# k weights as column halves around x of tile 3, a column of ones in the normalised tiles, and v weights less their row 512

## The chip, the cores and the metric

The kernel runs on one core of a Trainium2 chip. The metric is the device time of one execution in microseconds, as the median of several runs. Profiles come from one further execution that the hardware profiler recorded.

## The reference

The input x has 2048 rows of 640 values in bfloat16. The result is x plus two branches, and the second branch itself contains x again:

```python
def _A_ref(x, wqkv, wo):              # linear attention, 32 heads of 20
    qkv = (x @ wqkv) ...              # q, k, v
    phi = lambda t: jnp.where(t > 0, t + 1, jnp.exp(t)) + 1e-6
    pq, pk = phi(q), phi(k)
    kv = jnp.einsum("bhsd,bhse->bhde", pk, v)
    z = jnp.einsum("bhsd->bhd", pk)
    num = jnp.einsum("bhqd,bhde->bhqe", pq, kv)
    den = jnp.einsum("bhqd,bhd->bhq", pq, z)[..., None] + 1e-6
    return (num / den) ... @ wo

def _B_ref(x, w_r, w_gate, w_up, w_down):
    r = x @ w_r                       # the 8 rows of largest r go through
    idx = argsort(-r)[:8]             # a gated MLP, scaled by sigmoid(r)
    y = (silu(x[idx] @ w_gate) * (x[idx] @ w_up)) @ w_down * sigmoid(r[idx])
    return x + scatter_add(idx, y)

xn = _layernorm(x)
return x + _A_ref(xn, A_wqkv, A_wo) + _B_ref(xn, B_w_r, B_w_gate, B_w_up, B_w_down)
```

The layernorm has no gain and no bias: the 640 values of a normalised row add up to zero, apart from rounding.

## The kernel before

**Tiles.** The rows form 16 tiles of 128 (`T`), the 640 columns five chunks of 128 (`KC`). `XX[:, t, 1, :]` holds x of a tile, `XX[:, t, 0, :]` the normalised tile, `xnT` the normalised rows transposed, `pk` the feature map of k, `pqT` that of q, transposed. All of PSUM is one tile `PS` of eight banks, given out by hand.

**Engines and queues.** The order on each engine is the order of the program text (`manual_schedule`); waits between engines and for DMAs are derived from the tiles' accesses. PE multiplies, ACT does exponentials and copies, DVE the statistics, normalisation and elementwise work, POOL a square root for each tile (`ln_s`), masks and the gather of the selected rows. SP's queue issues nearly all loads and stores (`ld(sp, ...)`) and the DMA transposes (`tr_dma`).

**Start.** SP issues x of tiles 0, 1, 2, then the k weights `wk` in two parts, chunks 0 to 2 and 3 to 4, then x of tile 3 and of the rest. PE runs zero matmuls (`warm`) and transposes the router weights `w_r`, which ACT copies into column 640 of `wk` (L362, L364): so the second half of K also yields the router logits, 321 columns instead of 320. Tiles 0 to 3 are transposed on PE (`tr_pe`), later ones by DMA.

**k phase** (L339 to L445). `K(t)` multiplies tile t by the k weights in two halves of 320 columns (banks 6 and 7, ten matmuls), `PHa` takes exp and relu on ACT, `PHb` joins them into `pk` on DVE. `G(t)` (L261) accumulates G = xn^T pk over all tiles in banks 0 to 5, with the last 128 by 128 block done apart (`corner`, bank 6). The v projection isn't computed by rows: kv is later made from G and the v weights `wv` (`kv_pe`), in blocks along the diagonal. Iteration t of the loop runs K(t), PHb(t-1), the normalisation of tile t+2 with its DMA transpose, statistics of tile t+3 (`ln_a`, `ln_b`, `ln_g`, `ln_s`, `ln_c`), then G(t-1) and `loads(t)`: the q weights in five loads at 7 to 11, and at 13 the v weights in one, output weights, gate and up weights.

**q phase** (L465 to L825). `q_pe(tb, m, bank)` computes 128 columns of q for 512 rows, ACT takes exp and relu at once, `q_fin` joins them on DVE. Between these blocks stand: G's copies to SBUF, the routing of the eight rows (`route1` to `route3`), `kv_pe` and the masked evictions `kv_ev`, `zsum` (the sums of pk over all rows, by 64 matmuls with a tile of ones, into bank 2), `z_ev` and `z_mask`, which spread z over partitions, `m_tiled` and `m_full` (kv times the output weights), `den` (the denominators), the MLP (`gu_pe`, `ht_pe`, `y_pe`). `wd`, the down weights, uses the memory of `pk`, so it is loaded after pk's last reader.

**Output phase.** `out_mm(t)` and `out_ev(t)` for 16 tiles; the MLP's rows are added in DRAM by indirect DMAs.

Of the kernel before, what the change touches and what calls it, by code (L numbers as in the profile page):

```python
# [7 lines left out]
P = 128  # L8
S = 2048
D = 640  # L10
# [3 lines left out]
T = S // P  # L14
KC = D // P
# [8 lines left out]
EPS_BF16 = 1.0013580322265625e-05  # L24
LOW = S - 1
TF = 11

# [9 lines left out]
def kernel(  # L37
# [27 lines left out]
    def st(shape, dt, name, tag=None):  # L65
        return sb.tile(shape, dt, name=name, tag=tag or name)
# [4 lines left out]
    pqT = st([P, KC, S], BF16, "pqT")  # L71
    wk = st([P, KC, D + 1], BF16, "wk", "wkM")
    wq = st([P, KC, D], BF16, "wq")
# [21 lines left out]

    HW = 320


    def ld(eng, dst, src):
        eng.dma_start(dst, src)  # L100
# [8 lines left out]
    ld(sp, XX[:, 2, 1, :], x_v[:, 2, :])  # L109
    ld(sp, wk[:, 0:3, 0:D], wqkv_v[:, 0:3, D : 2 * D])  # L110
    ld(sp, wk[:, 3:KC, 0:D], wqkv_v[:, 3:KC, D : 2 * D])


    def warm(n, w=512):
        for _ in range(n):
            pe.matmul(PS[:, 7, 0:w], lhsT=zero[:, 0:P], rhs=zero[:, 0:w], start=True, stop=True)
# [40 lines left out]

    def ln_act(t):
        act.activation(junk[:], XX[:, t, 1, :], AF.Identity, scale=1.0 / D, accum_out=sm[:, t, 0:1])
        act.copy(MV[:, t, 0:1], sm[:, t, 0:1])  # L160
        act.activation(junk[:], XX[:, t, 1, :], AF.Square, scale=float(D) ** -0.5, accum_out=sm[:, t, 1:2])

    def ln_var(t):
# [55 lines left out]

    def K(t, hs=(0, 1), b=6, kcs=range(KC)):  # L220
        for h in hs:
            w = HW + h
            for kc in kcs:
                pe.matmul(  # L224
                    PS[:, b + h, off(t, h) : off(t, h) + w],
                    lhsT=xnT[:, kc, t * P : (t + 1) * P],
                    rhs=wk[:, kc, h * HW : h * HW + w],
                    start=(kc == 0),
                    stop=(kc == KC - 1),
                )  # L230
# [6 lines left out]
    def PHe(t, h, b=6):  # L237
        if h == 0:
            phis[t] = tuple(tmp.tile([P, D], BF16, tag=k, name=k, bufs=3) for k in ("ek", "rk"))
        act.activation(phis[t][0][:, h * HW : (h + 1) * HW], phi_src(t, h, b), AF.Exp)  # L240

    def PHr(t, h, b=6):
        act.activation(phis[t][1][:, h * HW : (h + 1) * HW], phi_src(t, h, b), AF.Relu)  # L243

# [12 lines left out]
    def PHb(t):  # L257
        ek, rk = phis[t]
        dve.scalar_tensor_tensor(out=pk[:, t, :], in0=ek[:], scalar=1.0, in1=rk[:], op0=ALU.min, op1=ALU.add)  # L259

    def G(t, ks=range(KC)):  # L261
        for a in ks:
# [5 lines left out]
            if a < 4:  # L268
# [3 lines left out]
                )  # L272

    def corner(t):
        pe.matmul(
            PS[:, 6, 0:P], lhsT=XX[:, t, 0, 512:D], rhs=pk[:, t, 512:D],
            start=(t == 0), stop=(t == T - 1), skip_group_check=True,
        )

    def zsum(b):  # L280
        for t in range(T):
            for j in range(4):
                pe.matmul(PS[32 * j : 32 * j + 32, b, 0:GC], lhsT=ones32[:], rhs=pk[:, t, j * GC : (j + 1) * GC],
                          start=(t == 0), stop=(t == T - 1), skip_group_check=True)

# [37 lines left out]
    def loads(t):  # L323
        if t < 5:
            ld(sp, XX[:, 6 + 2 * t : 8 + 2 * t, 1, :], x_v[:, 6 + 2 * t : 8 + 2 * t, :])
        if 7 <= t < 7 + KC:
            ld(sp, wq[:, t - 7, :], wqkv_v[:, t - 7, 0:D])
        if t == 13:
            ld(sp, wv[:], wqkv_v[:, :, 2 * D : 3 * D])
            ld(sp, wo1[:], wo_v[0:P, :, :])  # L330
            for g in range(NG):
                ld(sp, wo2[32 * g : 32 * g + 32, :], A_wo[GC * g + P : GC * (g + 1), :])
            for k in range(KC):
                ld(sp, wg[:, k, :], wg_v[:, k, :])
            for k in range(KC):
                ld(sp, wu[:, k, :], wu_v[:, k, :])

# [23 lines left out]
    ln_s(2)  # L361
    act.copy(wk[:, 0:3, D], PS[:, 5, :].bitcast(BF16)[:, 0:3])  # L362
    K(0, kcs=range(3))
    act.copy(wk[:, 3:KC, D], PS[:, 5, :].bitcast(BF16)[:, 3:KC])  # L364
# [17 lines left out]
    ln_g(3)  # L382
    ln_s(3)
    ln_c(3, dve)
    ln_a(4)
# [7 lines left out]
    ln_g(4)  # L393
    ln_s(4)
    PHr(2, 0)
    ln_c(4, dve)
# [19 lines left out]
    ln_s(6)  # L416
    ln_c(6, act)
    G(2)
    for t in range(4, T):
        K(t)  # L420
        PHb(t - 1)
        if t + 3 < T and t < 9:
            ln_a(t + 3)
        if t + 2 < T:
            ln_xn(t + 2)
            tr_dma(t + 2)
        PHa(t)
        if t + 3 < T:
            ln_b(t + 3)
            ln_g(t + 3)  # L430
            ln_s(t + 3)
# [12 lines left out]
        if t > 4:  # L444
            loads(t)  # L445
# [45 lines left out]

    zs = st([P, GC], F32, "zs")
# [276 lines left out]
    q_pe(1, 3, 2)  # L769
    z_mask()  # L770
# [8 lines left out]
    route3()  # L779
    q_pe(1, 4, 0)  # L780
    q_fin(1, 3)
    q_pe(2, 0, 1)
    q_fin(1, 4)
    q_pe(2, 1, 2)
    q_fin(2, 0)
# [7 lines left out]
    den_ev(1, 3)  # L793
    q_pe(2, 2, 0)
    q_fin(2, 1)
    q_pe(2, 3, 1)
    gu_ev(6)
    q_fin(2, 2)
    q_pe(2, 4, 2)
    ht_pe(4)  # L800
# [87 lines left out]
```

## Time and profile before

| | us |
|---|---|
| median of 3 runs (lowest, highest) | 113.0 (112.57, 113.93) |
| profiled execution | 113.0 |
| its span | 111.3 |
| PE busy | 103.7 |
| DVE busy | 84.1 |
| ACT busy | 75.9 |
| POOL busy | 21.6 |

The span runs from the first to the last instruction of the program; 1.7 us of the profiled execution lie outside it. Busy time of an engine leaves out its waits and the issue of DMAs. PE's row counts matmuls, weight loads are a row of their own and overlap it. A group is named by its line, so all K matmuls stand under L224, G under L264 and L269, q under L455, the output under L686.

### The profile page before, as it was taken

How to read it: one execution, taken by the hardware profiler on the slowest of the kernel's cores; microseconds unless marked ns; L12 is line 12 of the kernel's file. 1: busy time of each engine (PE TensorE's matmuls, PEld its weight loads, DVE VectorE, ACT ScalarE, POOL GpSimd, SP SyncE). 2: the span in 40 equal slices, each digit the busy share in tenths (PEclk: the TensorE clock that was granted, in tenths of full speed). 3: DMA queues.
4: the chain of work that ended last, by engine and by line, in shares of the span. 5: the costliest groups of instructions: out<-in, count | busy, mean ns of one | idle time of the engine just before them, and what ended most of it. 6: DMA issues, size and time to landing. Idle time of an engine off the chain costs nothing.

```text
span 111.3 us, 2742 instructions
## 1 busy us (share of the span) xinstructions
PE 103.7 (93%) x988; PEld 64.6 (58%) x998; DVE 84.1 (76%) x210; ACT 75.9 (68%) x168; POOL 21.6 (19%) x48
## 2 busy tenths in 40 slices
PE   5968998999999799999999999999999999999970
PEld 1236664666666466667557566565655767777740
DVE  1887987999999977755568976448869898689770
ACT  4626997887888778555496678999979965590000
POOL 7335112367442111000000012200006000000130
PEclk9999999999999999999999999999999999999999
DMA  3899920343356984379999707941721116389442
GB/s 87 231 350 379 238 55 20 62 60 62 66 125 143 77 181 112 66 200 379 358 395 402 276 6 218 382 131 32 251 83 48 32 33 247 62 239 378 162 133 82
DMA packets 22600, 19.04 MB, mean 171 GB/s; under 512 B 11194, under 2 KB 21306, under 8 KB 22586
## 3 DMA queue, kind: packets, MB, share of 16 engines
q1 hardware_dynamic: 21968, 18.69, 58.2%
q8 instruction: 8, 0.13, 0.6%
q10 hardware_dynamic: 330, 0.16, 0.5%
q0 software_dynamic: 288, 0.01, 0.3%
q14 instruction: 6, 0.05, 0.1%
HBM read 13.14 MB, written 3.65 MB: 151 GB/s over the span
## 4 chain that ended last, share of the span: by engine, by line
PE 62%; DMA 19%; DVE 9%; SPq 3%; ACT 2%; issue 2%; POOL 1%; DVEq 0%; ACTq 0%
PE PS L686 20%; PE PS L455 19%; DMA xnT<-XX 8%; PE PS L224 8%; DMA wo<-in_A_wo_dram 6%; PE PS L264 5%; DMA XX<-in_A_x_dram 5%; SPq L100 2%; DVE XX L186 2%; DVE pk L259 2%; PE PS L624 2%; PE PS L630 2%; PE PS L269 1%; PE PS L648 1%; DVE stats L148 1%
## 5 line engine op out<-in xcount | busy, mean ns | idle before, releaser
L224 PE MATMUL PS<-wk,xnT 128*128 128x320 bf16 (+1 forms) x160 | 24.9, 300 | 2.3 <-DMA xnT<-XX 0.9
L455 PE MATMUL PS<-xnT,wq 128*128 128x512 bf16 x95 | 22.8, 380 | 0.3
L264 PE MATMUL PS<-pk,XX 128*128 128x512 bf16 x75 | 22.4, 379 | 0.0
L686 PE MATMUL PS<-Mb,pqT 128*128 128x320 bf16 x160 | 22.1, 299 | 0.0
L224 PEld LDWEIGHTS <-xnT 128*128 128x128 bf16 x160 | 15.2, 97 | 10.3 <-DMA xnT<-XX 1.5
L240 ACT ACTIVATE ek<-PS 128x320 bf16<-128x320 f32 x32 | 14.6, 456 | 7.0 <-PE PS L224 7.0
L686 PEld LDWEIGHTS <-pqT 128*128 128x128 bf16 x160 | 15.5, 97 | 6.4
L172 POOL TENSOR_TENSOR s<-t,halfc 128x1 bf16<-128x1 bf16 x16 | 11.7, 732 | 26.4 <-DVE t L170 26.4
L455 PEld LDWEIGHTS <-wq 128*128 128x128 bf16 x100 | 11.4, 118 | 8.7
L510 DVE SCALAR_TENSOR_TENSOR pqT<-qe,qr 128x512 bf16<-128x512 bf16 x20 | 13.5, 683 | 3.7 <-ACT qr L462 3.7
L461 ACT ACTIVATE qe<-PS 128x512 bf16<-128x512 f32 x20 | 12.2, 608 | 5.5 <-PE PS L455 5.4
L700 DVE TENSOR_TENSOR o<-PS,XX 128x640 bf16<-128x640 f32 x15 | 12.3, 823 | 3.8 <-PE PS L686 2.1
L259 DVE SCALAR_TENSOR_TENSOR pk<-ek,rk 128x640 bf16<-128x640 bf16 x16 | 13.1, 818 | 2.7 <-ACT rk L243 2.7
L243 ACT ACTIVATE rk<-PS 128x320 bf16<-128x320 f32 x32 | 14.6, 458 | 0.0
L269 PE MATMUL PS<-pk,XX 128*128 128x128 bf16 x64 | 14.0, 219 | 0.3
L264 PEld LDWEIGHTS <-XX 128*128 128x128 bf16 x80 | 7.7, 98 | 8.0
L462 ACT ACTIVATE qr<-PS 128x512 bf16<-128x512 f32 x20 | 12.2, 608 | 0.0
L214 ACT ACTIVATE XX<-XX,MR,SR 128x640 bf16<-128x640 bf16 x11 | 9.4, 912 | 2.7 <-DVE pqT L544 2.7
L177 ACT ACTIVATE c<-XX,MVf 128x640 bf16<-128x640 bf16 x10 | 8.3, 832 | 1.2 <-DVE MVf L151 0.9
L145 DVE BATCH_NORM_STATS2 stats<-XX 128x6 f32<-128x320 bf16 x14 | 6.8, 488 | 2.6 <-DMA XX<-in_A_x_dram 2.6
L186 DVE TENSOR_SCALAR XX<-c,SR 128x640 bf16<-128x640 bf16 (+2 forms) x17 | 6.4, 383 | 1.3
L148 DVE BATCH_NORM_STATS2 stats<-XX 128x6 f32<-128x320 bf16 x14 | 6.8, 485 | 0.0
(118 smaller groups left out, 100.2 us busy)
## 6 DMA issues: line engine op xcount, KB each, us to landing
out_dram<-o SPq DMA_DIRECT2D x15, 160.0 KB, 3.3
XX<-in_A_x_dram SPq DMA_DIRECT2D x6, 320.0 KB, 6.4
wg<-in_B_w_gate_dram SPq DMA_DIRECT2D x5, 384.0 KB, 5.6
wu<-in_B_w_up_dram SPq DMA_DIRECT2D x5, 384.0 KB, 7.3
wd<-in_B_w_down_dram SPq DMA_DIRECT2D x1, 1920.0 KB, 9.5
wq<-in_A_wqkv_dram SPq DMA_DIRECT2D x5, 160.0 KB, 2.5
wv<-in_A_wqkv_dram SPq DMA_DIRECT2D x1, 800.0 KB
hi_d<-XX SPq DMA_DIRECT2D x1, 800.0 KB, 5.8
```

What stands on the lines that cost most here:

```text
L224: pe.matmul(PS[:, b + h, off(t, h) : off(t, h) + w], lhsT=xnT[:, kc, t * P : (t + 1) * P], rhs=wk[:, kc, h * HW : h * HW + w], start=(kc = ...
L240: act.activation(phis[t][0][:, h * HW : (h + 1) * HW], phi_src(t, h, b), AF.Exp)
L243: act.activation(phis[t][1][:, h * HW : (h + 1) * HW], phi_src(t, h, b), AF.Relu)
L259: dve.scalar_tensor_tensor(out=pk[:, t, :], in0=ek[:], scalar=1.0, in1=rk[:], op0=ALU.min, op1=ALU.add)
L264: pe.matmul(PS[:, a, :], lhsT=lhsT, rhs=pk[:, t, 0:512], start=(t == 0), stop=(t == T - 1),)
L269: pe.matmul(PS[:, 5, a * P : (a + 1) * P], lhsT=lhsT, rhs=pk[:, t, 512:D], start=(t == 0 and a == 0), stop=(t == T - 1), skip_group_check= ...
L455: pe.matmul(PS[:, bank, :], lhsT=by5(wq[:, kc, :])[:, m, :], rhs=xnT[:, kc, tb * TBLK : (tb + 1) * TBLK], start=(kc == 0), stop=(kc == KC ...
L461: act.activation(e, PS[:, bank, :], AF.Exp)
L462: act.activation(r, PS[:, bank, :], AF.Relu)
L510: dve.scalar_tensor_tensor(out=pqT[:, m, tb * TBLK : (tb + 1) * TBLK], in0=e, scalar=1.0, in1=r, op0=ALU.min, op1=ALU.add,)
L686: pe.matmul(PS[:, b + h, 0:HW], lhsT=pqT[:, kc, t * P : (t + 1) * P], rhs=Mb[:, kc, h * HW : (h + 1) * HW], start=(kc == 0), stop=(kc == K ...
L700: dve.tensor_tensor(out=ot[:].rearrange("p (h c) -> p h c", h=2), in0=PS[:, b : b + 2, 0:HW], in1=XX[:, t, 1, :].rearrange("p (h c) -> p h ...
```

## The change

1. `wk` becomes one flat tile with two views, `wkh[0]` (320 columns of each chunk) and `wkh[1]` (321). Each is loaded by a DMA of its own, with x of tile 3 between the two; rows of a load are 640 B where they were 1280 B. w_r goes into column 320 of `wkh[1]` ahead of that load, by one ACT copy. K of tile 0 runs the first half, then exp, then the transposes of tile 1, then the second half.
2. Of the warm-up matmuls in bfloat16 with 512 columns, eight become four in float32 with 256 (`warm4`). The transpose of w_r uses bank 3.
3. POOL sets column 512 of each normalised tile to one (`ones(t)`), after the tile has been transposed and ahead of `G(t)`. Row 512 of G is then the sum of pk, z. Since a normalised row adds up to zero, its value 512 is minus the sum of the others; so row 512 of the v weights is subtracted from all their rows (`wv_rows`, on DVE, in iterations 11 to 15, with `wvb`, that row broadcast), and kv comes out as before. `zsum` and its ones tile go; `z_ev` copies 512 and 128 values of one partition and needs one DMA instead of four, right after `route1`.
4. Loads: the v weights take the q weights' place in iterations 7 to 11, the q weights the v weights' place at 13 in one load, the up weights go behind `z_ev`.
5. `ln_a(t+4)` stands at the end of an iteration from 4 on, where that began at 8. `q_pe(1, 1)` moves ahead of `m_tiled(0)`, and the banks of some later q blocks change. `ACTS` is empty, so its branches do nothing.

```diff
+ZD = 4 * P
+ACTS = ()
-    wk = st([P, KC, D + 1], BF16, "wk", "wkM")
+    wk = st([P, KC * (D + 1)], BF16, "wk", "wkM")
-    ones32 = st([P, 32], BF16, "ones32")
+    wvb = st([P, D], BF16, "wvb")
+    wkh = [wk[:, 0 : KC * HW].rearrange("p (k c) -> p k c", k=KC),
+           wk[:, KC * HW : KC * (D + 1)].rearrange("p (k c) -> p k c", k=KC)]
-    ld(sp, wk[:, 0:3, 0:D], wqkv_v[:, 0:3, D : 2 * D])
-    ld(sp, wk[:, 3:KC, 0:D], wqkv_v[:, 3:KC, D : 2 * D])
+    ld(sp, wkh[0], wqkv_v[:, :, D : D + HW])
+    ld(sp, XX[:, 3, 1, :], x_v[:, 3, :])
+    zero32 = zero[:].bitcast(F32)
+    def warm4(n):
+        for _ in range(n):
+            pe.matmul(PS[:, 7, 0:256], lhsT=zero32[:, 0:P], rhs=zero32[:, 0:256], start=True, stop=True)
-    dve.memset(ones32[:], 1.0)
-    warm(4)
-    pe.transpose(PS[:, 5, :].bitcast(BF16)[:, 0:KC], wr[:], ident[0:KC, 0:KC])
-    warm(5)
-    ld(sp, XX[:, 3, 1, :], x_v[:, 3, :])
+    warm4(2)
+    pe.transpose(PS[:, 3, :].bitcast(BF16)[:, 0:KC], wr[:], ident[0:KC, 0:KC])
+    warm4(2)
+    warm(1)
+    act.copy(wkh[1][:, :, HW], PS[:, 3, :].bitcast(BF16)[:, 0:KC])
+    ld(sp, wkh[1][:, :, 0:HW], wqkv_v[:, :, D + HW : 2 * D])
...
-                    rhs=wk[:, kc, h * HW : h * HW + w],
+                    rhs=wkh[h][:, kc, 0:w],
+    def ones(t):
+        pool.memset(XX[:, t, 0, ZD : ZD + 1], 1.0)
+    def wv_rows(k):
+        dve.tensor_tensor(out=wv[:, k, :], in0=wv[:, k, :], in1=wvb[:], op=ALU.subtract)
-    def zsum(b):
-        for t in range(T):
-            for j in range(4):
-                pe.matmul(PS[32 * j : 32 * j + 32, b, 0:GC], lhsT=ones32[:], rhs=pk[:, t, j * GC : (j + 1) * GC],
-                          start=(t == 0), stop=(t == T - 1), skip_group_check=True)
...
         if 7 <= t < 7 + KC:
-            ld(sp, wq[:, t - 7, :], wqkv_v[:, t - 7, 0:D])
+            ld(sp, wv[:, t - 7, :], wqkv_v[:, t - 7, 2 * D : 3 * D])
+        if t == 6:
+            ld(sp, wvb[:], A_wqkv[ZD : ZD + 1, 2 * D : 3 * D].to_broadcast([P, D]))
         if t == 13:
-            ld(sp, wv[:], wqkv_v[:, :, 2 * D : 3 * D])
+            ld(sp, wq[:], wqkv_v[:, :, 0:D])
...
-            for k in range(KC):
-                ld(sp, wu[:, k, :], wu_v[:, k, :])
...
-    act.copy(wk[:, 0:3, D], PS[:, 5, :].bitcast(BF16)[:, 0:3])
-    K(0, kcs=range(3))
-    act.copy(wk[:, 3:KC, D], PS[:, 5, :].bitcast(BF16)[:, 3:KC])
+    ones(0)
+    K(0, (0,))
+    PHe(0, 0)
     tr_pe(1, 2, act, act)
-    K(0, kcs=range(3, KC))
-    PHe(0, 0)
     consts_e()
     bm2_copies(sp, (1, 2))
     PHr(0, 0)
+    K(0, (1,))
...
+    ones(1)
...
+    ones(2)
...
+    ones(3)
     G(2)
     for t in range(4, T):
         K(t)
+        ones(t)
         PHb(t - 1)
-        if t + 3 < T and t < 9:
+        if t + 3 < T and t < 5 and t + 3 not in ACTS:
             ln_a(t + 3)
...
-        if t + 4 < T and t >= 8:
+        if t + 4 < T and t >= 5 - 1 and t + 4 not in ACTS:
             ln_a(t + 4)
...
+        if t > 10:
+            wv_rows(t - 11)
         G(t - 1)
...
-    def z_ev(b):
-        dve.tensor_copy(zs[:], PS[:, b, 0:GC])
-        for j in range(4):
-            ld(sp, zcol[32 * j : 32 * j + 32, :], zs[32 * j : 32 * j + 1, :])
+    def z_ev():
+        dve.tensor_copy(zs[:, 0:512], PS[0:1, 4, :])
+        dve.tensor_copy(zs[:, 512:D], PS[0:1, 6, 0:P])
+        ld(sp, zcol[:], zs[:])
...
     route1()
+    z_ev()
+    for k in range(KC):
+        ld(sp, wu[:, k, :], wu_v[:, k, :])
...
     kv_pe(3)
-    zsum(2)
     kv_ev(3)
     q_pe(0, 4, 0)
-    z_ev(2)
...
+    q_pe(1, 1, 2)
     m_tiled(0, 6)
     m_tiled(1, 4)
     m_full(0, 6, dve)
     m_full(1, 4, act)
-    q_pe(1, 1, 0)
     q_fin(1, 0)
-    q_pe(1, 2, 1)
+    q_pe(1, 2, 0)
...
```

More of the change, by code (lines that the diff above doesn't have):

```diff
@@ L156, with ln_act1, ln_act2, ln_act @@
     junk = st([P, D], BF16, "junk")
-    def ln_act(t):
+    def ln_act1(t):
         act.activation(junk[:], XX[:, t, 1, :], AF.Identity, scale=1.0 / D, accum_out=sm[:, t, 0:1])
         act.copy(MV[:, t, 0:1], sm[:, t, 0:1])
+    def ln_act2(t):
         act.activation(junk[:], XX[:, t, 1, :], AF.Square, scale=float(D) ** -0.5, accum_out=sm[:, t, 1:2])
+    def ln_act(t):
+        ln_act1(t)
+        ln_act2(t)
     def ln_var(t):
@@ L218, in off, with K @@
         return T - 1 - t if t != 1 and h else 0
-    def K(t, hs=(0, 1), b=6, kcs=range(KC)):
+    def K(t, hs=(0, 1), b=6):
         for h in hs:
             w = HW + h
-            for kc in kcs:
+            for kc in range(KC):
                 pe.matmul(
@@ L428 @@
         if t + 3 < T:
-            ln_b(t + 3)
-            ln_g(t + 3)
-            ln_s(t + 3)
+            if t + 3 in ACTS:
+                ln_act2(t + 3)
+                ln_var(t + 3)
+                ln_s(t + 3, -1.0)
+            else:
+                ln_b(t + 3)
+                ln_g(t + 3)
+                ln_s(t + 3)
             ln_c(t + 3, act)
-        if t + 4 < T and t >= 8:
+        if t + 4 < T and t + 4 in ACTS:
+            ln_act1(t + 4)
+        if t + 4 < T and t >= 5 - 1 and t + 4 not in ACTS:
             ln_a(t + 4)
@@ L490 @@
     dve.tensor_copy(Gs[:, 4, 512:D], PS[:, 6, 0:P])
-    zs = st([P, GC], F32, "zs")
+    zs = st([1, D], F32, "zs")
     zcol = st([P, KC], F32, "zcol")
     zm = st([P, KC, 32], BF16, "zm")
-    def z_ev(b):
-        dve.tensor_copy(zs[:], PS[:, b, 0:GC])
-        for j in range(4):
-            ld(sp, zcol[32 * j : 32 * j + 32, :], zs[32 * j : 32 * j + 1, :])
+    def z_ev():
+        dve.tensor_copy(zs[:, 0:512], PS[0:1, 4, :])
+        dve.tensor_copy(zs[:, 512:D], PS[0:1, 6, 0:P])
+        ld(sp, zcol[:], zs[:])
     def z_mask():
@@ L764 @@
     m_full(1, 4, act)
-    q_pe(1, 1, 0)
     q_fin(1, 0)
-    q_pe(1, 2, 1)
+    q_pe(1, 2, 0)
     q_fin(1, 1)
-    q_pe(1, 3, 2)
+    q_pe(1, 3, 1)
     z_mask()
@@ L779 @@
     route3()
-    q_pe(1, 4, 0)
+    q_pe(1, 4, 2)
     q_fin(1, 3)
-    q_pe(2, 0, 1)
+    q_pe(2, 0, 0)
     q_fin(1, 4)
-    q_pe(2, 1, 2)
+    q_pe(2, 1, 1)
     q_fin(2, 0)
@@ L793 @@
     den_ev(1, 3)
-    q_pe(2, 2, 0)
+    q_pe(2, 2, 2)
     q_fin(2, 1)
-    q_pe(2, 3, 1)
+    q_pe(2, 3, 0)
     gu_ev(6)
     q_fin(2, 2)
-    q_pe(2, 4, 2)
+    q_pe(2, 4, 1)
     ht_pe(4)
```

## The prediction

> **What bounds the kernel now.** I read the page's busy shares first, then a table by stage, then the chain that ended last, then the order of time of each engine around every wait of that chain.
>
> ```profile
> span 111.3 us, 2742 instructions
> PE 103.7 (93%) x988; PEld 64.6 (58%) x998; DVE 84.1 (76%) x210; ACT 75.9 (68%) x168; POOL 21.6 (19%) x48
> ...
> PE   5968998999999799999999999999999999999970
> ...
> 60.97:85.57 24.60, 24.39 (x279) 14.41 (x284) 17.86 (x43) 20.99 (x45) 2.97 (x9) 1.00 0.50 164
> ```
>
> The third line is PE's busy share in tenths, in 40 slices of 2.8 us; the fourth is the stage from zsum's end to the output phase: length, busy time of PE, PEld, DVE, ACT and POOL, granted clock (1.00), DMA share and GB/s. From the fifth slice to the last but one PE hardly rests: TensorE's own work sets the time, and whoever takes work or a wait out of PE's row shortens the kernel by it. There are few waits. In PE's order of time these stand out:
>
> ```profile
> 7.55 0.57 PE L224 MATMUL PS<-wk,xnT 128*128 128x320 bf16 x3 [0.67 <-DMA wk<-in_A_wqkv_dram]
> 8.68 0.57 PE L224 MATMUL PS<-wk,xnT 128*128 128x321 bf16 x3 [0.56 <-ACT wk L364]
> ...
> 9.37 1.48 PE L224 MATMUL PS<-wk,xnT 128*128 128x320 bf16 x9
> ...
> 18.71 0.38 PE L264 MATMUL PS<-pk,XX 128*128 128x512 bf16 x1
> 19.45 1.54 PE L224 MATMUL PS<-wk,xnT 128*128 128x320 bf16 x10 [0.36 <-DMA xnT<-XX]
> ...
> 38.81 1.54 PE L224 MATMUL PS<-wk,xnT 128*128 128x320 bf16 x10 [0.52 <-DMA xnT<-XX]
> ...
> 53.00 1.24 PE L455 MATMUL PS<-xnT,wq 128*128 128x512 bf16 x4
> ```
>
> The rows at 19.45 and 38.81 are K of tiles 4 and 11, each waiting for its DMA transpose. The chain tells where these come from and what one block of the change is worth:
>
> ```profile
> 3.19 5.62 DMA XX<-in_A_x_dram
> ...
> 14.89 4.51 DMA xnT<-XX
> 19.40 0.05 issue
> ...
> 34.48 4.29 DMA xnT<-XX
> ...
> 59.85 1.12 PE PS L283 x64
> ```
>
> The first row is x of tile 3, which landed at 8.81; the transpose of tile 4 hangs on it.
>
> **Term 1, the 64 sums of `zsum`.** All are removed: 1.12 us of PE by the chain's row, with PE busy on both sides. z comes instead from row 512 of G, which the same matmuls of `G` and `corner` write as before, only with a one in the column. Does the time close up, or does ACT fill it?
>
> ```profile
> 59.54 0.73 ACT L462 ACTIVATE qr<-PS 128x512 bf16<-128x512 f32 x1
> 62.21 0.60 ACT L461 ACTIVATE qe<-PS 128x512 bf16<-128x512 f32 x1 [1.95 <-PE PS L455]
> ```
>
> ACT had read the banks by 60.27 and stood idle 1.95 us until the next q block. With that block 1.12 us earlier, 0.83 us of idle time is left, so ACT does not bind here; over 60.97 to 85.57 it is busy 20.99 of 24.60 us. The mask multiplies (`kv_ev`), which `m_tiled` needs, keep their place on DVE, and the change puts `q_pe(1, 1)` ahead of `m_tiled` in just the gap that zsum had covered. I take the full -1.12 (ends: 0 if the next stage is bound by something else, -1.12).
>
> **Term 2, the start.** The SP queue now takes x0, x1, x2, half of wk, x3, the other half.
>
> ```profile
> 8.83 0.49 DVE L145 BATCH_NORM_STATS2 stats<-XX 128x6 f32<-128x320 bf16 x1 [0.65 <-DMA XX<-in_A_x_dram]
> ...
> 10.86 0.49 DVE L145 BATCH_NORM_STATS2 stats<-XX 128x6 f32<-128x320 bf16 x1
> ...
> 8.46 0.17 ACT L362 COPY wk<-PS 128x3 bf16<-128x3 bf16 x1 [1.37 <-DMA wk<-in_A_wqkv_dram]
> ```
>
> The first part of wk (480 KB) was there at 7.55, the second (320 KB) at 8.46, x3 (160 KB) at 8.81: about 0.9 us for 320 KB and 0.35 to 0.45 for a tile of x. Each half is now 400 KB: the first 0.2 us earlier, about 7.3; x3 at 7.75; the second half at 8.9. Its 640 B rows are new here; I allow up to 0.4 us more, 9.3. DVE is free at 8.18, so the statistics of tile 3, and with them the whole chain to the transpose of tile 4, start 0.65 us earlier: landing 19.40 - 0.65 = 18.75, if the transfer is as long. The second half waits on SP for ACT's copy of w_r; behind it stand the loads of x4 to x15, some 0.4 us later. The first of them to be read is x4, at 10.86 or 0.65 before; by the same bytes at the same rate it is there by about 10.
>
> PE: K(0) of the first half starts at 7.4 and no longer waits for ACT to copy w_r behind a landing; that copy now stands ahead of the second load, in ACT's wait for x of tile 1. The second half of K(0) starts at about 9.0 and ends at 9.7, where it ended at 9.37 + 4 x 0.137 = 9.92 before (0.137 is one of ten from the rows at 1.54). PE was ready for K(4) at 18.71 + 0.22 = 18.93, and would be at 18.7, so 18.8 is taken: -0.65. Ends: 0 (a late half of wk, or the old landing), and -1.0 if the transpose lands early and ACT, freed of its idle time, lets PE run from 9.4.
>
> ```profile
> 16.00:17.00 1.00, 1.00 0.83 164
> 17.00:18.00 1.00, 1.00 0.06 17
> 18.00:19.00 1.00, 1.00 0.00 0
> ...
> xnT<-XX SPq DMA_TRANSPOSE x12, 2.6
> ```
>
> These rows (last columns: DMA share and GB/s) are why the ends lie far apart: the 160 KB of tile 4 were moved by 18 at the latest and the DMAs then idle, yet the landing was told at 19.40; other transposes landed in 2.6 us. Such a late landing may fall elsewhere next time.
>
> A page of the Trainium skill speaks against the halves: "DMA: Bandwidth & Descriptors", section "How a descriptor splits into AXI transactions", says that a descriptor which doesn't start at a multiple of 256 B fetches bytes that it doesn't use. By it the second half, whose rows start at byte 1920, costs 24 beats a row where 20 would do, an estimated 0.2 us later, and the sum would be some 0.1 us smaller. No run here shows it yet.
>
> **Term 3, K of tile 11.** From `t` = 5 on `ln_a(t+4)` stands behind `ln_s`, and the iteration with two of them moves from 8 to 4.
>
> ```profile
> 30.01 0.81 DVE L259 SCALAR_TENSOR_TENSOR pk<-ek,rk 128x640 bf16<-128x640 bf16 x1
> 33.07 0.81 DVE L259 SCALAR_TENSOR_TENSOR pk<-ek,rk 128x640 bf16<-128x640 bf16 x1
> 35.60 0.81 DVE L259 SCALAR_TENSOR_TENSOR pk<-ek,rk 128x640 bf16<-128x640 bf16 x1
> ```
>
> DVE's iteration took 3.06 us with two of them and 2.53 in the new order, against PE's 2.67. The surplus at 4 is made good by 0.14 us an iteration before 8, so normalised tile 11 and its transpose come about 0.45 us earlier, and of the 0.52 us wait I take -0.45 (ends 0 and -0.52).
>
> **What is added, at nothing.** (a) `wv_rows`, five on DVE in iterations 11 to 15, and `z_ev`, larger and earlier:
>
> ```profile
> L544 DVE TENSOR_TENSOR pqT<-pqT,R 128x1280 bf16<-128x1280 bf16 x8 | 6.5, 816 | 0.0
> L485 DVE CAST Gs<-PS 128x512 bf16<-128x512 f32 x1 | 0.7, 692 | 1.2 <-PE PS L264 1.2
> L490 DVE CAST Gs<-PS 128x128 bf16<-128x128 f32 x1 | 0.3, 280 | 0.0
> L118 POOL MEMSET halfc<- 128x1 bf16 x1 | 0.1, 101 | 0.3 <-POOLq L872 0.3
> ...
> 41.22 0.83 DVE L259 SCALAR_TENSOR_TENSOR pk<-ek,rk 128x640 bf16<-128x640 bf16 x1 [0.47 <-ACT rk L243]
> 49.23 0.82 DVE L259 SCALAR_TENSOR_TENSOR pk<-ek,rk 128x640 bf16<-128x640 bf16 x1 [1.13 <-ACT rk L243]
> 58.34 0.69 DVE L510 SCALAR_TENSOR_TENSOR pqT<-qe,qr 128x512 bf16<-128x512 bf16 x1 [1.06 <-ACT qr L462]
> ```
>
> One subtraction is half of the 816 ns, 0.41 us; the upper bound is L259's 0.82. DVE's waits for ACT of 0.47 to 1.13 us an iteration cover the 0.41; at 0.82 `pk` would come up to 0.4 us late, which G reads only after K, 1.4 us of PE work. `z_ev` costs 0.69 + 0.28 = 0.97 and has the 1.06 us wait before 58.34. (b) Sixteen one-column memsets on POOL, 0.1 us each, ahead of the square roots; each waits for its tile's transpose, which K also needs, and G reads column 512 an iteration later. Lower bound 0; upper bound 16 waits of PE at 0.05 us (a released engine's "issue" in the chain), 0.8. I take 0. (c) The float32 warm-up: four of 256 columns for eight of 512, taken as the same time. (d) DMAs: `wvb` and the five v loads stand where five q loads stood, gate weights keep their place, up weights go behind `z_ev`. SP waits there for the small z load's data, with up and down weights queued behind; even in the 9.5 us that wd took, they land before the gate and up matmuls, which stand behind ten more q blocks. The q weights become one 800 KB load, in v's old slot:
>
> ```profile
> 46.56 0.57 SPq L100 DMA_DIRECT2D wv<-in_A_wqkv_dram  x1
> 51.54 0.33 SPq L100 DMA_DIRECT2D wg<-in_B_w_gate_dram  x1
> SPq L100 <- DMA wv<-in_A_wqkv_dram: 0.7, 1, 0.7
> wd<-in_B_w_down_dram SPq DMA_DIRECT2D x1, 1920.0 KB, 9.5
> ```
>
> SP waited for v's landing before its issue at 51.54, so v came 4.95 us after its issue; the first q matmul comes at 53.00. So q has 1.4 us to spare.
>
> **Sum.** -1.12 - 0.65 - 0.45 = -2.2 us. The profiled execution is 113.0 us, its span 111.3, and 113.0 is also the median of the runs (112.57 to 113.93). Forecast: span 109.1, time 110.8.
>
> **Rivals.**
> *Only zsum goes.* Both waits of K were late landings, which needn't follow the issue. For it: the idle DMA rows at 17 to 19. Against: both transposes are issued earlier. 113.0 - 1.12 = 111.9.
> *zsum was cover.* ACT, at 20.99 of 24.60 us, becomes the bound of the q phase; terms 2 and 3 alone: 111.9. Against: its idle 1.95 us.
> *No late landing.* K(4) follows PE's work at once: 113.0 - 1.12 - 1.0 - 0.52 = 110.4.
> *A colder TensorE.* If the float32 warm-up keeps PE less busy, the first matmuls run at half rate:
>
> ```profile
> 1.24 1.89 PE L116 MATMUL PS<-zero 128*128 128x512 bf16 x4 [1.24 <-DVE MVf L105]
> ```
>
> These lie 0.43 us apart (less the last one's 0.6), where 512 columns at the 0.137 of 320 are 0.22. Four such us from K(0) on cost 2 us: 112.8. The Trainium skill ("TensorE: Matmul & The Clock Gate", section "What's actually happening") also says that the clock is released only after some 3.4 us of activity; the early rows agree with a slow start.
> *Slower: q comes late.* It decides from 6.4 us after issue, and the kernel is slower than before from 8.7. At wd's 9.5 us PE would wait 3.1: 113.9. Against it: the 4.95 us of the same load in the same slot.
>
> **Numbers.** Forecast 0.45 (its own range 110.0 to 111.4), only zsum 0.20, cover 0.07, no late landing 0.17, cold 0.05, q late 0.06. Range 109.9 to 112.8: it leaves out late q and the far ends of the others. Two per cent (2.26 us, about what a measurement of this kernel can tell from no change) lies at 110.7, inside the forecast's own range: a little over half of it (0.25) and all of "no late landing" (0.17) fall below, 0.42. Slower by over 2% needs q beyond wd's time: most of its 0.06, say 0.05. Within: 0.53.
>
> **What would show it.** Right: no L283; stage from q's start to the output phase 1.1 us shorter; x3's statistics at about 8.2; K(4) at 18.8 or before; no wait at K(11). Wrong: a PE wait for `wq` near 52, waits of G for POOL, ACT's idle time gone in the q phase, K(0)'s matmuls 0.27 apart.

## The result and the profile after

| | before | after |
|---|---|---|
| median of 6 runs each (lowest, highest), us | 112.78 (112.20, 113.93) | 110.91 (110.43, 110.94) |
| ratio of the two, 95% interval | | 0.984 (0.981 to 0.988) |
| profiled execution, us | 113.0 | 110.71 |
| its span, us | 111.3 | 109.0 |

The change makes the kernel 1.87 us faster by the medians, 1.6% by the ratio: the forecast was 110.8 and a span of 109.1. Ratios, here and below, leave out the few executions whose granted clock was low and whose time was longer; medians and ranges keep them. The head of the page after (span, busy time of each engine, PE's 40 slices) shows the same picture as before, shorter; TensorE still sets the time.

```profile
span 109.0 us, 2635 instructions
PE 102.7 (94%) x934; PEld 64.9 (60%) x934; DVE 86.3 (79%) x215; ACT 75.6 (69%) x167; POOL 22.0 (20%) x64
...
PE   5978997999999999999999999999999999999980
```

PE's order of time after, at the same places as in the prediction: the first half of K(0), its second half (in one row with the first half of K(1)), the end of G ahead of K(4), K(4), the end of G ahead of K(11), K(11), the first q block, and the first q block after `kv_pe` (the last row).

```profile
6.72 0.85 PE L241 MATMUL PS<-wk,xnT 128*128 128x320 bf16 x5 [0.21 <-ACT xnT L214]
8.54 1.53 PE L241 MATMUL PS<-wk,xnT 128*128 128x321 bf16 x10 [0.43 <-DMA wk<-in_A_wqkv_dram]
...
17.65 0.38 PE L281 MATMUL PS<-pk,XX 128*128 128x512 bf16 x1
18.76 1.55 PE L241 MATMUL PS<-wk,xnT 128*128 128x320 bf16 x10 [0.73 <-DMA xnT<-XX]
...
37.27 0.38 PE L281 MATMUL PS<-pk,XX 128*128 128x512 bf16 x1
37.74 1.55 PE L241 MATMUL PS<-wk,xnT 128*128 128x320 bf16 x10
...
51.96 1.24 PE L484 MATMUL PS<-xnT,wq 128*128 128x512 bf16 x5
58.75 3.43 PE L484 MATMUL PS<-xnT,wq 128*128 128x512 bf16 x15
```

Set against the rows of before, K(4) starts at 18.76 for 19.45 (-0.69), K(11) at 37.74 for 38.81 (-1.07, so -0.38 between the two), q at 51.96 for 53.00 (-1.04, nothing since K(11)). The sums of `zsum` are gone. The table by stage (length, busy time of PE, PEld, DVE, ACT, POOL, granted clock, DMA share, GB/s) has the rest:

```profile
57.84:58.81 0.97, 0.97 (x102) 0.94 (x102) 0.68 (x2) 0.97 (x3) 0.00 (x0) 1.00 0.12 22
58.81:83.51 24.70, 24.70 (x284) 14.51 (x284) 18.62 (x45) 21.43 (x46) 4.39 (x9) 1.00 0.64 209
```

The first row is `kv_pe`; the next q block follows it, where zsum stood. The second row is the stage that was 24.60 us long: 24.70 now. So 0.69 + 0.38 + 1.12 = 2.2 of the span's 2.3 us lie where the prediction put them. Whether they came about as it said is another matter: K(4) waits for its transpose longer than before (0.73, it was 0.36).

### The profile page after: what moved, and what is told of

Same layout as the page of the kernel before. It is cut to its first block, busy times and chain, and to the rows that moved or that the text cites. A ratio compares the mean times of both kernels' runs of the same rounds, so it can differ in the third digit from the quotient of the medians.

```text
span 109.0 us, 2635 instructions
## 1 busy us (share of the span) xinstructions
PE 102.7 (94%) x934; PEld 64.9 (60%) x934; DVE 86.3 (79%) x215; ACT 75.6 (69%) x167; POOL 22.0 (20%) x64
## 4 chain that ended last, share of the span: by engine, by line
PE 73%; DMA 10%; DVE 8%; POOL 3%; ACT 1%; issue 1%; DVEq 0%; ACTq 0%
PE PS L484 20%; PE PS L715 20%; PE PS L241 12%; PE PS L281 10%; DMA xnT<-XX 8%; POOL s L189 3%; DVE XX L203 2%; DMA XX<-in_A_x_dram 2%; PE PS L286 2%; PE PS L653 2%; PE PS L659 2%; PE PS L677 1%; DVE pk L276 1%; DVE stats L159 1%; PE PS L547 1%
## 5 line engine op out<-in xcount | busy, mean ns | idle before, releaser
L281 PE MATMUL PS<-pk,XX 128*128 128x512 bf16 x80 | 23.2, 379 | 0.0
L189 POOL TENSOR_TENSOR s<-t,halfc 128x1 bf16<-128x1 bf16 x16 | 9.9, 618 | 26.1 <-DVE t L187 26.1
L281 PEld LDWEIGHTS <-XX 128*128 128x128 bf16 x80 | 7.7, 98 | 8.1
L156 DVE BATCH_NORM_STATS2 stats<-XX 128x6 f32<-128x320 bf16 x14 | 6.8, 486 | 1.9 <-DMA XX<-in_A_x_dram 1.9
L286 PEld LDWEIGHTS <-XX 128*128 128x128 bf16 x64 | 6.2, 97 | 0.9
```

The source lines that it names most:

```text
L189: pool.tensor_tensor(out=ss[t][:], in0=t2[:], in1=halfc[:], op=ALU.pow)
L281: pe.matmul(PS[:, a, :], lhsT=lhsT, rhs=pk[:, t, 0:512], start=(t == 0), stop=(t == T - 1),)
L286: pe.matmul(PS[:, 5, a * P : (a + 1) * P], lhsT=lhsT, rhs=pk[:, t, 512:D], start=(t == 0 and a == 0), stop=(t == T - 1), skip_group_check= ...
```

## The experiments

All were timed over five rounds with before beside them, in four groups, each on one chip: the repeat of the change, the sums, x of tile 3 and the narrow warm-ups; the old start, the old order, nothing added and the 15 split matmuls; the 35 split ones with a second repeat; z alone. "The change" means the kernel after.

### Undoing the parts

**The change once more**, as the yardstick of its group.

> The kernel of the change itself, run beside the others. Both theories: 110.9 us, K of tile 4 at 18.8 us after a wait of 0.7, K of tile 11 after a wait of about 0.3.

Measured: 110.93 (110.16 to 111.49), ratio 0.982 (0.977 to 0.987). The profile differs from the first in its start:

```profile
7.25 1.08 PE L241 MATMUL PS<-wk,xnT 128*128 128x320 bf16 x5
...
19.27 0.31 PE L241 MATMUL PS<-wk,xnT 128*128 128x320 bf16 x1 [0.87 <-DMA xnT<-XX]
```

K(0) came 0.53 us later, its five matmuls took 1.08 for 0.85, and K(4) came at 19.27 for 18.76. Half a microsecond at the start is the difference between two executions of one kernel; a single profile can't weigh the start's terms.

**The 64 sums put back**, into bank 5, their result unused:

```
     kv_pe(3)
+    zsum(5)      # 4 x 16 matmuls, ones32 against pk
```

> The changed kernel with the 64 sums put back on TensorE behind kv_pe, into bank 5; their result is not used. If they lay on the path (term 1): 1.1 us longer, 112.0, and ACT's wait for the next q block back from 0.83 to 1.95 us. If the q phase is bound by ACT or by its banks: less than 0.5 us longer.

Measured: 111.74 (111.33 to 112.02), 0.81 more than the change. In the profile:

```profile
58.03 0.81 PE L635 MATMUL PS<-Gs,wv 128*32 128x40 bf16 x80
...
58.83 1.30 PE L308 MATMUL PS<-pk,ones 128*32 128x160 bf16 x64
60.06 0.63 PE L492 MATMUL PS<-xnT,wq 128*128 128x512 bf16 x2
```

From `kv_pe` at 58.03 to the next q block are 2.03 us; in the repeat of the change, whose rows follow, 0.90 (58.23 to 59.13). The difference is 1.13. From there to the output phase both take the same time (24.59 and 24.60), and ACT's wait for the q block is back at 1.95 us, as expected. So the block costs what its chain row said, and nothing of it is made up later: term 1 stands, and "zsum was cover" falls.

```profile
58.23 0.81 PE L627 MATMUL PS<-Gs,wv 128*32 128x40 bf16 x80
...
59.13 0.84 PE L484 MATMUL PS<-xnT,wq 128*128 128x512 bf16 x3
```

**x of tile 3 behind the second half of wk**:

```
     ld(sp, wkh[0], ...)
-    ld(sp, XX[:, 3, 1, :], x_v[:, 3, :])
     ...
     ld(sp, wkh[1][:, :, 0:HW], ...)
+    ld(sp, XX[:, 3, 1, :], x_v[:, 3, :])
```

> The changed kernel with x of tile 3 loaded behind both halves of wk. Chain theory (the transpose of tile 4 lands a fixed 4.2 us after its issue, and its issue follows from x3): x3 at about 8.9, the issue 0.5 later, K(4) at 19.3, 111.4 us. Packet theory (the landing is held up by a 16 KB packet of TensorE's instruction stream, which starts at 17.4 us in the trace of before and at 16.7 in that of after, 2.0 us ahead of the landing both times; its time depends on how far TensorE has come): K(4) where it was or up to 0.4 us earlier, since the second half of K(0) starts earlier; 110.5 to 110.9 us.

Measured: 111.62 (111.23 to 111.99), 0.69 more. The profile doesn't show where:

```profile
8.97 0.49 DVE L156 BATCH_NORM_STATS2 stats<-XX 128x6 f32<-128x320 bf16 x1 [0.79 <-DMA XX<-in_A_x_dram]
...
15.03 1.21 SPq L219 DMA_TRANSPOSE xnT<-XX  x1
...
19.36 0.31 PE L241 MATMUL PS<-wk,xnT 128*128 128x320 bf16 x1 [0.81 <-DMA xnT<-XX]
```

The statistics of tile 3 are late and wait for x, as meant. In the repeat of the change the same three steps come at 8.48, 14.87 and 19.27, in the first profile after at 8.11, 14.50 and 18.76. So 0.49 us at the statistics arrive as 0.16 at the issue and 0.09 at K(4). That speaks against x3 as the cause of K(4)'s time, while the median, above both expectations, speaks for a cost that these rows don't hold. The profiled executions can't show it: this one, at 111.23, was the fastest of its six, and the repeat's, at 111.14, was slower than the repeat's median. Left open.

```profile
8.48 0.48 DVE L156 BATCH_NORM_STATS2 stats<-XX 128x6 f32<-128x320 bf16 x1
...
14.87 1.21 SPq L219 DMA_TRANSPOSE xnT<-XX  x1
```

**The old start, the old order of `ln_a`, and nothing added**, three kernels of one group. The first has wk by rows of chunks, the bf16 warm-ups and x3 behind wk, as before:

```
-    ld(sp, wkh[0], wqkv_v[:, :, D : D + HW])
+    ld(sp, wk[:, 0:3, 0:D], wqkv_v[:, 0:3, D : 2 * D])
+    ld(sp, wk[:, 3:KC, 0:D], wqkv_v[:, 3:KC, D : 2 * D])
     ld(sp, XX[:, 3, 1, :], x_v[:, 3, :])
```

> The changed kernel with the start of before: wk in two groups of chunks ahead of x of tile 3, K of tile 0 in the order of before, bfloat16 warm-up. If the new start is worth term 2: 0.65 us longer, 111.6, K(4) at about 19.4. If only z and the order of the statistics count: 110.9.

The second:

```
-        if t + 3 < T and t < 5 and t + 3 not in ACTS:
+        if t + 3 < T and t < 9 and t + 3 not in ACTS:
...
-        if t + 4 < T and t >= 5 - 1 and t + 4 not in ACTS:
+        if t + 4 < T and t >= 8 and t + 4 not in ACTS:
```

> The changed kernel with ln_a in its places of before (two in iteration 8). Term 3: the transpose of tile 11 issued about 0.4 us later against TensorE, its wait back to about 0.5 us, 0.2 to 0.4 us longer: 111.2. If only the packet sets that wait: its landing follows the packet at about 36 us and not its issue, no change, 110.9.

The third leaves out the memsets of column 512 and `wv_rows`, so its row 512 of G is not z:

> The changed kernel without the sixteen one-column memsets on POOL and without wv_rows on DVE: the sums z and the correction of the v weights are left out (and eps of the denominator is 1e6, so that its logarithm stays defined). If the added work lies under other work: 110.9, within 0.2. If G waits for POOL, or DVE delays the transposes: 0.3 to 0.8 shorter.

| kernel | median (lowest, highest) | ratio to before (95%) |
|---|---|---|
| old start | 111.11 (110.68, 112.33) | 0.988 (0.985 to 0.992) |
| old order of `ln_a` | 111.28 (110.82, 111.84) | 0.992 (0.989 to 0.995) |
| nothing added | 110.98 (110.75, 114.03) | 0.989 (0.986 to 0.993) |

Against the change's 110.9, the additions cost nothing, as forecast; the order is worth 0.36 us, where 0.2 to 0.4 was expected, and the start 0.2. The change itself wasn't timed in that group: beside the kernel with nothing added, which was, the two are 0.30 and 0.13. All of these are less than what medians of one kernel differ by between groups (before had 112.57 to 113.16), so the medians alone settle neither. With the old order K(11) waits 37.83 - (37.18 + 0.22) = 0.43 us, where the first profile of the change has 0.25; with the old start K(4) waits 1.02 us:

```profile
37.18 0.38 PE L281 MATMUL PS<-pk,XX 128*128 128x512 bf16 x1
37.83 1.41 PE L241 MATMUL PS<-wk,xnT 128*128 128x320 bf16 x9 [0.27 <-DMA xnT<-XX]
```

```profile
14.84 4.50 DMA xnT<-XX
19.38 1.54 PE PS L237 x10
```

The second fence is the chain of waits with the old start. The transpose of tile 4 was issued at 14.84, as in the change's repeat (14.87), and landed at 19.34 (there 19.22). The front moved things, but K(4) hangs on a landing that takes 4.2 to 4.5 us each time, where the median transpose takes 2.6. What makes this one late?

### The late transposes

The packets of every DMA queue in the trace show it. Each transpose is told as landed by sixteen signals. In the profile after, fifteen of tile 4 had come by 17.13, 2.63 us after the issue; the last came at 18.71. On queue q8 of the page after (packets, MB, share of 16 engines) seven packets of kind "instruction" lie in the whole execution, 16 KB each:

```profile
q8 instruction: 7, 0.11, 0.4%
```

The first two of them and the transposes of the k phase that took over 3.5 us, from the trace's records:

```
kernel        packet at  transpose issued, landed     packet at  transpose issued, landed
before        17.38      tile 4   14.89 19.40 (4.51)  35.70      tile 11  34.48 38.77 (4.29)
after         16.70      tile 4   14.50 18.71 (4.21)  35.52      tile 11  33.28 37.70 (4.42)
its repeat    16.96      tile 4   14.87 19.22 (4.35)  36.04      tile 11  33.79 38.08 (4.29)
old start     17.33      tile 4   14.84 19.34 (4.50)  35.99      tile 11  33.88 38.21 (4.33)
old order     16.36      tile 4   14.19 18.62 (4.43)  35.26      tile 11  33.92 37.79 (3.87)
```

No other transpose of a tile in these five executions took over 3.25 us. So the theory: these packets bring in a piece of TensorE's program, and the transpose that is in flight then lands 2 to 3.1 us after the packet. The number of packets fits: the two kernels with the 64 sums (before, and the one with the sums put back) have eight on q8, the twelve others seven. The Trainium skill ("DMA: Bandwidth & Descriptors", section "Queues, rings and completion order") says that each DMA engine takes turns between its queues and drains a whole packet of one before it turns to the next. Tile 4's transpose in the profile after agrees, with one signal of sixteen late; but the packet takes 0.93 us there and the delay is 1.6 (4.21 for 2.6), and tile 11's transpose in the same profile doesn't agree: all sixteen of its signals came late, from 37.52 to 37.70. So the rule may explain one form of the delay, not both.

Nor do these rows say whether the landing keeps time with the packet or with the issue. In the nine kernels and repeats that leave the first packet between 16.3 and 17.4 us and tile 4's transpose late, that landing comes 4.2 to 4.5 us after the issue and 2.0 to 2.3 us after the packet; both fit as well. The packet has to be moved away from the transpose.

If the packets follow PE's own place in its program, more PE instructions early on bring them forward. Three attempts.

**Narrower warm-ups**, 24 of 128 columns in bf16 for the four in float32:

```
-    warm4(2)
+    warm(12, 128)
     pe.transpose(PS[:, 3, :]..., wr[:], ident[0:KC, 0:KC])
-    warm4(2)
+    warm(12, 128)
```

> The changed kernel with the four float32 warm-up matmuls replaced by 24 bfloat16 ones of 128 columns: the same 3.6 us of warm-up, 32 more rows in TensorE's instruction stream ahead of tile 0. Packet theory: at some 14 rows a us the packets come 2.3 us earlier, at 14.4 and 33.2 us, before the transfers of the transposes of tiles 4 and 11; K(4) at 18.0 without a wait, none at K(11), 1.0 us shorter: 109.9. Chain theory: no change, 110.9.

Measured: 111.25 (110.47 to 111.57), 0.32 more than the change beside it, with overlapping ranges. A miss of the 109.9. One reason isn't in the theory: the warm-ups were over too soon, PE stood idle for 1.27 us, and K(0) ran slowly.

```profile
3.26 1.59 PE L126 MATMUL PS<-zero 128*128 128x128 bf16 x9
6.12 0.71 PE L210 MATMUL PS<-ident,XX 128*128 128x128 bf16 x5 [1.27 <-DVE XX L203]
...
7.20 1.51 PE L241 MATMUL PS<-wk,xnT 128*128 128x320 bf16 x5
```

Five matmuls of K(0) took 1.51 us, 0.85 after the change. This is the prediction's "colder TensorE", shown in a kernel that brings it about; whether the idle time or the narrow matmuls bring it about isn't told apart, and the row of granted clock in this kernel's page, nines over the whole start, doesn't show it. By the Trainium skill ("TensorE: Matmul & The Clock Gate", section "What's actually happening") the clock is let go by some 3.4 us of activity, and how many matmuls run cold varies from run to run of one kernel; the 0.85, 1.08 and 0.85 of the three profiles of the change agree with that. The packets did come earlier, at 15.74 and 33.70 (14.4 and 33.2 were expected); tile 4 landed in 3.88 us at 18.71, just as PE was ready for it, and the second late transpose was now that of tile 10, with K(10) waiting 0.47:

```profile
31.43 4.30 DMA xnT<-XX
35.78 1.55 PE PS L241 x10
```

**Split matmuls.** The 15 K matmuls of tile 0 and of the first half of tile 1 in two parts each, of 160 columns and the rest, which is as much streaming and 30 more instructions:

```
+                parts = ((0, 160), (160, w)) if t == 0 or (t == 1 and h == 0) else ((0, w),)
+                for c0, c1 in parts:
                     pe.matmul(PS[:, b + h, o + c0 : o + c1], ..., rhs=wkh[h][:, kc, c0:c1], ...)
```

> The changed kernel with 15 of its first 20 K matmuls (tile 0, and the first half of tile 1) split into two of half the columns each: 30 more rows in TensorE's instruction stream at nearly no time, the warm-up untouched. Packet theory: the 16 KB instruction packets of TensorE come some 2 us earlier, at about 14.6 and 33.4 us, neither within the transfer of a transpose; tile 4 lands 2.6 us after its issue, K(4) starts without a wait (18.0 to 18.4), no wait at K(10) or K(11): about 0.8 us shorter, 110.1. Chain theory: the wait of 0.7 to 0.9 at K(4) stays, 110.9.

Measured: 110.61 (110.32 to 111.13). That is 0.3 less than the change's 110.9, which was timed in other groups, and 0.37 less than the kernel with nothing added, in the same group; the ratio to before, 0.985 (0.982 to 0.989), is no better than the change's. So a gain isn't shown, and 110.1 was missed. K(4) no longer waits; the second wait has moved to K(10), as with the narrow warm-ups:

```profile
18.24 1.54 PE L244 MATMUL PS<-wk,xnT 128*128 128x320 bf16 x10
...
35.28 0.99 PE L244 MATMUL PS<-wk,xnT 128*128 128x320 bf16 x6 [0.47 <-DMA xnT<-XX]
```

**More of them.** If the first packet comes before tile 4's transpose is issued, that one should land in 2.6 us. The K matmuls of tiles 0, 1, 5 and the first half of 2 are split, once in the change and once with the old start.

```
-                parts = ((0, 160), (160, w)) if t == 0 or (t == 1 and h == 0) else ((0, w),)
+                parts = ((0, 160), (160, w)) if t in (0, 1, 5) or (t == 2 and h == 0) else ((0, w),)
```

> The changed kernel with K of tiles 0, 1 and 5 and the first half of tile 2 split in two by columns: 50 more rows in TensorE's stream ahead of the first 16 KB instruction packet, 70 ahead of the second. In split30 the packets came at 15.7 and 33.2 us and held tiles 4 and 10. Now about 14.8 and 31.2, each between the landing of one transpose and the transfer of the next. Packet theory: all twelve transposes land 2.6 to 3.3 us after their issue, K(4) at 18.0 to 18.4 and no wait at K(10) or K(11): 110.1 us. If a packet only picks another tile: about 110.6 as with split30.

> The start of before with the split of split70, so that no instruction packet holds the transpose of tile 4. If the new start is worth the 0.65 us of term 2 once the landing is free: 0.65 longer than split70, 110.75. If it is worth the 0.2 us that front_back showed: 110.3.

The yardstick of this group is the change again:

> The kernel of the change once more beside the next two: 110.9 us.

| kernel | median (lowest, highest) | ratio to before (95%) |
|---|---|---|
| the change | 110.82 (110.58, 111.17) | 0.977 (0.974 to 0.981) |
| 35 split | 111.56 (110.92, 112.21) | 0.984 (0.979 to 0.988) |
| old start, 35 split | 111.51 (110.94, 111.77) | 0.982 (0.978 to 0.986) |

As times both are misses: 0.7 us more than the change, where less was expected. As a test of the mechanism they are the clearest of all, with one profile each:

```
kernel                packet at  tile 4 issued, landed  packet at  the late one
narrow warm-ups       15.74      14.83 18.71 (3.88)     33.70      tile 10  31.43 35.73 (4.30)
15 split              15.74      14.58 18.19 (3.61)     33.18      tile 10  30.93 35.24 (4.31)
35 split              14.83      14.54 17.66 (3.12)     31.32      tile 9   29.27 33.55 (4.28)
old start, 35 split   14.14      14.64 17.21 (2.57)     31.39      tile 9   28.76 33.42 (4.66)
```

In the first two rows all sixteen signals of tile 4 came late, within 0.13 us of each other; of tiles 10 and 9 one signal in sixteen did.

With the old start and 35 splits the first packet is there before tile 4's transpose is issued, and the transpose takes the usual 2.57; K(4) starts at 18.53 without a wait, 0.85 us earlier than with the old start alone. The second packet then hits tile 9:

```profile
18.31 0.38 PE L281 MATMUL PS<-pk,XX 128*128 128x512 bf16 x1
18.53 1.53 PE L240 MATMUL PS<-wk,xnT 128*128 128x320 bf16 x10
...
32.11 0.38 PE L281 MATMUL PS<-pk,XX 128*128 128x512 bf16 x1
33.47 1.54 PE L240 MATMUL PS<-wk,xnT 128*128 128x320 bf16 x10 [0.98 <-DMA xnT<-XX]
```

PE could have begun K(9) at 32.11 + 0.22 = 32.33, the same 0.22 as before the waits of the prediction, and began 1.14 us later: all the gain at K(4) is given back, and more. Some of the gain was lost before that. K(5), in twenty parts, takes 1.46 us for 1.36 (21.29 to 22.75). And once K(4) doesn't wait, PE runs into the next limit: after K(6), which isn't split, G begins 0.28 us late (24.05 to 25.69, where 1.36 would do), just as DVE ends the `pk` that it reads (24.83 + 0.81 = 25.64).

```profile
24.83 0.81 DVE L276 SCALAR_TENSOR_TENSOR pk<-ek,rk 128x640 bf16<-128x640 bf16 x1
...
25.69 0.38 PE L281 MATMUL PS<-pk,XX 128*128 128x512 bf16 x1
```

The kernel with the narrow warm-ups, which splits nothing, has the same 0.28 at that place. So even with every transpose on time, not all of K(4)'s wait could have been saved. From tile 7 on the transposes follow each other with hardly a gap, so a packet there meets one, and the earlier tile has a little less to spare (in the profile after, tile 9 landed 1.46 us ahead of its K, tile 10 1.63). In the kernel with 35 splits in the change, the second half of wk also came late in the profile (a wait of 1.45 us at 9.76, 0.43 after the change), and K(9) waited:

```profile
9.76 1.57 PE L244 MATMUL PS<-wk,xnT 128*128 128x160 bf16 x20 [1.45 <-DMA wk<-in_A_wqkv_dram]
...
33.59 1.55 PE L244 MATMUL PS<-wk,xnT 128*128 128x320 bf16 x10 [0.59 <-DMA xnT<-XX]
```

On the start's worth, which this pair was also to tell, neither expectation came true: with the same splits the old start is 0.05 us shorter than the new one. But the second packet holds tile 9 in both, so the pair can't weigh the start.

### Only z

Last, the old start and the old order together, with only the z part of the change kept, to see whether the parts add up.

> The start of before (wk in row blocks, bf16 warm-up) and its order of ln_a, with only the z part of the change kept. If the parts add up as their single undoings say (start 0.2, order 0.36), it is at about 111.5. If both waits are late landings that follow nothing the change moved, so that z alone is the change's worth (rival 'only zsum goes', read strictly: before minus 1.12 = 111.9 and the kernel with all parts no faster), it ties with the whole change at about 110.9. If the parts of the start and of the order are worth the forecast's 0.65 and 0.45, it is at 112.0. Waits: K(4) should wait about as in before (landing about 19.4, an instruction packet at about 17.3), and tile 11's transpose should be late again, with a packet at about 35.5 to 36.

Measured: 111.75 (110.99 to 112.56) beside 112.82 of before on the same chip, ratio 0.992 (0.988 to 0.995). So z alone brings 1.07 us by the medians and 0.95 by the ratio, near the 1.12 of its row; the whole change brings 1.87, and the start and the order together the other 0.8. One by one, undoing them gave 0.2 and 0.36, and the 0.3 between is inside what these medians can't tell: the time lies between the expectations of 111.5 (the single undoings) and 112.0 (the forecast's terms). In this profile the clock that TensorE was granted fell in the third and fourth slice, 5.5 to 11 us:

```profile
PEclk9985999999999999999999999999999999999998
...
19.30 0.38 PE L277 MATMUL PS<-pk,XX 128*128 128x512 bf16 x1
19.52 0.71 PE L237 MATMUL PS<-wk,xnT 128*128 128x320 bf16 x4
```

PE came to K(4) at 19.52 without any wait, against what was expected: the first packet (17.43) fell into the transpose of 15.13 and didn't delay it (landed 17.69, 2.56). So overlap alone isn't enough. Nor was this transpose too near its end to be held: the packet came 2.30 us after its issue here, and 2.49 after it in before and with the old start, where the landing was late all the same. What decides is open. The second packet, at 36.56, again fell into tile 11's transpose (35.46 to 39.30, 3.84), and K(11) waited:

```profile
39.35 0.85 PE L237 MATMUL PS<-wk,xnT 128*128 128x320 bf16 x5 [0.30 <-DMA xnT<-XX]
```

## Why the prediction was right, and where it was not

**Term 1 (-1.12) was right** in place and size: 1.13 in the profile with the sums put back, 0.81 and 1.07 by the two pairs of medians. ACT's idle time after it is the 0.83 us that was worked out:

```profile
58.51 0.72 ACT L491 ACTIVATE qr<-PS 128x512 bf16<-128x512 f32 x1
60.06 0.60 ACT L490 ACTIVATE qe<-PS 128x512 bf16<-128x512 f32 x1 [0.83 <-PE PS L484]
```

For the two waits of K, one profile of each kernel is a small sample. The profiles of the change and its two repeats, beside before and the old order (waits by the starts: K's start less the last G's start and 0.22):

```
                   K(4) at   K(11) at   between   wait of K(4)   of K(11)
before             19.45     38.81      19.36     0.52           0.68
the change         18.76     37.74      18.98     0.89           0.25
its repeat         19.27     38.13      18.86     1.03           0.12
its 2nd repeat     18.89     38.18      19.29     0.51           0.56
old order          18.67     37.83      19.16     0.95           0.43
```

**Term 2 (-0.65) came out at -0.69 in the first profile, by another road and partly by luck.** The two repeats have -0.18 and -0.56. The early steps were right: the statistics of tile 3 come at 8.11, without a wait (forecast 8.2).

```profile
8.11 0.49 DVE L156 BATCH_NORM_STATS2 stats<-XX 128x6 f32<-128x320 bf16 x1
...
14.50 1.21 SPq L219 DMA_TRANSPOSE xnT<-XX  x1
```

The step that failed is the next one, "with them the whole chain to the transpose of tile 4": 0.72 us at the statistics became 0.39 at the issue (14.89 to 14.50), because the way between them took 6.39 for 6.06 us. DVE works without a pause there: after tile 3's first statistics the reciprocal for tile 2 follows 0.12 us later than in before, and the step that writes normalised tile 2 takes 0.59 us for 0.39 (0.59 in the repeats too, 0.39 to 0.50 in the kernels with the old start); why is open. The landing moved by 0.69, nearly as the packet did (17.38 to 16.70, 0.68); whether the packet's move or the issue's set that number isn't shown. PE was ready for K(4) at 17.65 + 0.22 = 17.87, 1.06 us earlier than the 18.93 of before: the far end of the term, -1.0, is what PE gained, and the late landing kept 0.4 of it. By medians the start is worth 0.2 to 0.5 (the latter from 111.75 - 110.91 = 0.84, less the order's 0.36). The profiles say much the same: K(4) came at 19.45 in before and 19.38 with the old start put back, and at 18.67 to 19.27, 18.96 in the mean, in the six profiles that leave the new start as it is. So the term was too large, and the doubt that stood beside the forecast, that a late landing needn't follow the issue, was right: with the packet moved, tile 4 landed 2.57 to 3.88 us after its issue, where it took 4.2 to 4.5. It was put as a rival ("only zsum goes", 111.9); the time of that rival is what z alone gave, 111.75, not the change.

**Term 3 (-0.45)** is 0.38 between K(4) and K(11) in the first profile and 0.36 by the median. Its step holds: tile 11's transpose is issued 14.5 to 14.7 us after K(4) starts in the change and its repeats, and 15.03 (before) and 15.25 (old order) without the term. The time from K(4) to K(11) is 19.36 and 19.16 with the old order; in seven profiles with the new one (the change, its two repeats, the sums put back, x of tile 3 late, the old start, nothing added) it is 18.73 to 18.98 in six and 19.29 in one, the second repeat. So its size is 0.2 to 0.6, and in one execution it wasn't there. The wait isn't wholly gone: 37.27 + 0.22 = 37.49 to 37.74 are 0.25 us, too short for the brackets of the view. The transpose of tile 11 is issued 1.2 us earlier than before (33.28, it was 34.48), 0.69 of that the start's; it is late all the same, landing at 37.70.

```profile
33.28 4.42 DMA xnT<-XX
37.74 1.55 PE PS L241 x10
```

**What was added, at nothing**: right by the median without it (110.98). POOL's memsets of the column wait for transposes, 3.9 us in all, and nobody on PE waits for them. The q weights, one load now, were needed at 51.96 and landed at 50.51, 5.0 us after their issue, where 4.95 was forecast:

```profile
POOL XX L292 <- DMA xnT<-XX: 3.9, 3, 2.6
...
45.50 0.57 SPq L104 DMA_DIRECT2D wq<-in_A_wqkv_dram  x1
```

**The halves of wk.** Whether the second half's rows cost the 0.2 us that the prediction weighed can't be told here: that half was waited for until 8.54 in the first profile, 9.11 in the second repeat and 9.76 in another kernel with the same loads, a spread of six times the 0.2 us at stake.

**The sum** held because its largest term was read from a row of PE with PE busy on both sides; the two smaller terms each came out within 0.1 in the first profile, but the start's by a mechanism that was not the one stated, and smaller by the medians. Part of the closeness is luck: at K(11) the change was ahead of before by 1.07 us in that profile, but by 0.68 and 0.63 in the repeats, where 1.10 was forecast. And the time of 110.8 was hit to 0.1 from a starting point of 113.0; six runs put that at 112.78, so of the 2.2 us forecast 1.87 were measured.

## What to carry to other kernels

A block of matmuls with PE busy on both sides is worth its own row in the chain; a wait at the end of a transfer is worth what ends the transfer, so look first at why that one took 4.5 us where its like take 2.6. If the late one moves to another tile when instructions are added, it is bound to the program's position and not to the load, and shifting it only helps where the tile that it hits next has more to spare. Where two executions of one kernel differ by half a microsecond at the start, a term of that size needs several profiles, or medians taken beside the unchanged kernel in the same group; one profile doesn't settle it.

## What was not expected of the hardware

Pieces of TensorE's program arrive during the execution in packets of 16 KB, 16 to 19 us apart in the k phase, each 0.9 to 1.5 us long; a DMA transpose that one falls into lands 3.1 to 4.7 us after its issue in place of 2.6. In one execution it didn't (2.56), and why is open. Sometimes one of its sixteen signals is late, sometimes all are. Thirty more matmul and weight-load instructions brought the first packet from 16.70 to 16.96 in the profiles of the change to 15.74. Halving a K matmul costs little: ten of 320 columns lie 0.137 us apart and twenty of 160 lie 0.070 apart, and K of a tile takes 1.46 us for 1.36.
